# Attention and MoE on one core: the first group's q and k rows, its masks and its weight requests rearranged

## The chip, the cores and the metric

The kernel runs on one core of a Trainium2 chip. The metric is device time in microseconds (us) for one launch, as the median of several runs. Engines are named as the profile names them: PE is TensorE (PEld its weight loads), DVE is VectorE, ACT is ScalarE, POOL is GpSimd, SP is SyncE. POOL and SP, and in the beginning ACT too, also issue transfers (DMAs).

## What is computed

Two steps in a row: attention over 4 batches, 8 heads, 768 tokens and 64 values a head, then a mixture of four experts over the 3072 rows of 512 that come out. Heads 0, 2 and 6 attend to all earlier tokens; heads 1, 3, 4, 5 and 7 attend to the first 4 tokens (sinks) and to a window of 64.

```python
def _attn_ref(q, k, v, is_retrieval, n_sink, window):
    B, H, S, D = q.shape                    # 4, 8, 768, 64
    scores = np.matmul(q, k.transpose(0, 1, 3, 2)) / np.sqrt(D)
    pos = np.arange(S)
    rel = pos[:, None] - pos[None, :]
    causal = rel >= 0
    is_sink = pos[None, :] < int(n_sink)                    # 4
    in_win = (rel >= 0) & (rel < int(window))               # 64
    stream_keep = causal & (is_sink | in_win)
    ...                                     # mask: causal or stream_keep, by head
    a = np.exp(scores - np.max(scores, axis=-1, keepdims=True))
    a = a / (np.sum(a, axis=-1, keepdims=True) + 1e-09)
    return np.matmul(a, v)

def _moe_ref(x, domain_probs, w1, w2):      # x 3072 x 512, w1 4 x 512 x 1024
    p = domain_probs / (domain_probs.sum(-1, keepdims=True) + 1e-09)
    out = np.zeros((N, D))
    for e in range(E):                      # 4 experts
        h = np.maximum(x @ w1[e], 0.0)
        out += p[:, e:e + 1] * (h @ w2[e])
    return out
```

Inputs and output are float32; the kernel computes in fp16 with float32 accumulation.

## The kernel before

Work is cut into eight groups of 384 tokens, half a batch each. For every group the attention runs first and leaves `xT`, the 512 attention values of the group's tokens transposed as four pieces of 128 rows (one for each pair of heads); the MoE of that group reads `xT`. From group 1 on, attention is interleaved with the MoE of earlier groups. Group 0 has nothing to be interleaved with: its attention (`attention(0, 0)`, called "first" in the code) runs alone at the start, and this is the stretch that the change touches. The schedule is manual: each engine executes its instructions in the order in which the source issues them, and Python generators (`yield from`) write that order out. POOL's own order is also the order of the transfers that it requests, as all of them go through one queue.

**Loads of group 0.** The q and k rows of all eight heads come as float32. For each head one DMA of 96 KB brings q and one brings k (L411, L424), in runs of 256 bytes (one row of a head): partition p gets the rows p, 128 + p and 256 + p. SP issues all of k and q of heads 4 to 7; ACT's queue issues q of heads 0 to 3. They land in `hA`, the tile that later holds the hidden layer.

**POOL at the start.** It makes the identity for transposes, requests the values of head 0, and makes the bias masks: `bC` (causal, L457 and L459) and `bS` (window and sinks, three blocks of 160 columns; memset L467, two selects of 2 x 160 columns L468 and L472, small parts L476 to L478, copy of a block L509). Then it requests the values of heads 2, 1, 3, 4, 6, 5 and 7 (`load_v`, L304 for the full heads and L310 for the stream heads), then w1 of expert 0 in two halves of 512 KB (`load_w1`, L335; one half is contraction rows for 64 of the 128 partitions, so every matmul needs both), then w2 of expert 0, and w1 of expert 1. A tiny copy, `landed` (L521), makes POOL wait until a tensor is there; after it come the next q and k rows (L230) and w2 and w1 of the next experts.

**Transposes.** TensorE transposes q and k for each pair of heads `hp` (`transposes(hp)`, heads 2hp and 2hp + 1): three transposes of 128x128 float32 for q, three for k (L576; later groups use pairs of fp16 matmuls with 64 columns, L579). q goes to `qT` by one copy (ACT for the first two pairs, DVE for the others); k goes to `kR` (full heads, L602) or `kS` (stream heads, L618, with the sinks' keys by L626), by DVE. `kS` and `kR` are zeroed first (L379, on DVE).

**Scores and values.** Scores are matmuls (L693), the bias mask is added by a matmul with the identity (L705), ACT takes the exponential into `es` (L711). Values times `es` are matmuls (L756 for full heads, L828 for stream heads), which also give the sums; ACT makes the reciprocal by Ln (L846) and Exp (L856, L861), and DVE multiplies it in (L851), which writes a piece of `xT`. Pairs with a full head go through `x_transposes` (L805, then the copy L809). The order of TensorE in group 0 is

```python
            yield from both(scores(1), values(0))
            yield from transposes(2)
            yield from both(scores(3), values(2))
            x_transposes(0)
            yield from scores(4)
            yield from transposes(3)
            yield from values(1)
            yield from both(scores(5), values(3))
```

after transposes and scores of pairs 0 and 1, and before the scores and values of heads 5, 6 and 7. Matmuls on zeros (`warm_up`, L448) fill some of the waits of TensorE. The first MoE matmuls (L1095, x times w1 of expert 0, pieces of `xT` in the order 0, 2, 1, 3) follow; L1116 is the second layer with w2.

Of the kernel before, what the change touches and what calls it, by code (L numbers as in the profile page):

```python
# [11 lines left out]
FP32 = mybir.dt.float32  # L12
# [7 lines left out]
def kernel(  # L20
# [311 lines left out]
    def load_w1(e, f0, f1):  # L332
        x = moe_w1[e].rearrange("(u c d) f -> u d c f", u=2, c=DMP)
        for u in range(2):
            gp.dma_start(  # L335
                out=w1sb[half(u), e * DMP : (e + 1) * DMP, f0:f1],
                in_=x[u, :, :, f0:f1],
            )
# [42 lines left out]
    def zero(eng, t):  # L381
        fill(eng, t.rearrange("p a b x -> p (a b x)"), 0.0)
# [17 lines left out]
    def rows32(n):  # L400
        x = hA[:, n * 6 * H * D : (n + 1) * 6 * H * D].bitcast(FP32)
        return x.rearrange("p (j h d) -> p j h d", j=3, h=H)
# [3 lines left out]
    for h in range(H):  # L406
        if h == 2:
            nc.sync.dma_start(
                out=v_s32, in_=v[0, :, 0:NS, :].rearrange("h r d -> r h d")
            )  # L410
        nc.sync.dma_start(out=k32[:, :, h, :], in_=rows_of(k, 0, h, 0))  # L411
        if h == HP:

            nc.scalar.add_instruction(
                mybir.InstLoadActFuncSet(
                    name=nc.get_next_instruction_name(),
                    engine=ENG.Activation,
                    act_func_set_id=[x.name for x in SETS].index(
                        "natural_log_exp_and_others"
                    ),  # L420
                )
            )
        eng = nc.scalar if h < HP else nc.sync
        eng.dma_start(out=q32[:, :, h, :], in_=rows_of(q, 0, h, 0))  # L424
# [8 lines left out]
    nc.vector.memset(warm.bitcast(FP32), 0.0)  # L433
    nc.vector.memset(eps, 1e-9)
# [5 lines left out]
    zero(nc.vector, kS[:, 0, :, :, :])  # L440
# [14 lines left out]
    def mask_c(x, keep, drop):  # L455

        gp.memset(x, keep)  # L457
# [7 lines left out]
    def mask_s(x, n, keep, drop):  # L465

        gp.memset(x, keep)  # L467
        gp.affine_select(  # L468
            out=x, in_=x, compare_op=ALU.is_ge, fill=drop,
            base=R0, pattern=[[0, n], [1, TQ]], channel_multiplier=-1,  # L470
        )
        gp.affine_select(  # L472
            out=x, in_=x, compare_op=ALU.is_ge, fill=drop,
            base=NW - 1 - R0, pattern=[[0, n], [-1, TQ]], channel_multiplier=1,
        )
        gp.memset(x[0:R0, :, :], drop)  # L476
        gp.memset(x[0:NS, :, 0:TK], keep)
# [28 lines left out]

    mask_c(bC, 0.0, -60000.0)
    mask_s(bS[:, 0:2, :], 2, 0.0, -60000.0)
    gp.tensor_copy(out=bS[:, 2, :], in_=bS[:, 1, :])  # L509
    load_v(0, 0, [2, 1, 3, 4, 6, 5, 7])  # L510
    load_w1(0, 0, F)
# [46 lines left out]
    def attention(b, c):  # L558
# [8 lines left out]
        def transposed(x, hp):  # L567
# [5 lines left out]
            for j in range(3):  # L573
                o = ps[:, j * P : (j + 1) * P]
                if first:
                    nc.tensor.transpose(o, x[:, j, 2 * hp : 2 * hp + 2, :], ident32)  # L576
                    continue
                for u in range(2):
                    nc.tensor.matmul(  # L579
                        out=o[u * D : (u + 1) * D, :],  # L580
                        lhsT=x[:, 2 * hp + u, j, :],
                        rhs=ident16,
# [5 lines left out]
        def transposes(hp):  # L588
            both_at_once = [] if first else [transposed(x, hp) for x in (qt16, k16)]
            for x, is_k in ((q32 if first else qt16, 0), (k32 if first else k16, 1)):  # L590
                ps = transposed(x, hp) if first else both_at_once[is_k]
# [288 lines left out]
        if first:  # L880
# [8 lines left out]
            sink_row(7)  # L889
            yield from both(scores(1), values(0))  # L890
            yield from transposes(2)
            yield from both(scores(3), values(2))
            x_transposes(0)
            yield from scores(4)
            yield from transposes(3)
            yield from values(1)
            yield from both(scores(5), values(3))
# [770 lines left out]
```

## Time and profile before

| what | value |
|---|---|
| median of 3 runs | 376.53 us (376.28 to 376.87) |
| the profiled execution | 377.82 us, its span 376.1 us |
| granted TensorE clock | 1.00 |
| PE busy | 367.1 us, 98% of the span, 4221 instructions |
| PEld busy | 312.4 us, 83% |
| DVE busy | 281.6 us, 75% |
| ACT busy | 227.3 us, 60% |
| POOL busy | 112.9 us, 30% |
| DMA | 39.25 MB, mean 104 GB/s |

The span is the stretch in which the engines work; the execution's own time lies 1.7 us above it. Times inside a span are counted from its start. "Idle before" in a row is the time that the engine stood still ahead of an instruction, and the arrow names what released it. A row "x3" stands for three neighbours of one line and form. Matmuls are pipelined: one row's time may overlap the next row's start, so the price of a group of matmuls is read from start to start.

### The profile page before, as it was taken

To read this page: it belongs to the slowest core of one execution; us is meant where nothing else is said; L and a number is where in the kernel's file an instruction comes from. 1 tells how busy PE (TensorE), PEld (TensorE's weight loads), DVE (VectorE), ACT (ScalarE), POOL (GpSimd) and SP (SyncE) were. 2 spreads that over 40 slices of the span, in tenths; PEclk is the share of its full clock that TensorE was granted. 3 is DMA by queue.
4 is the path that set the end of the run, shared out by engine and by line. 5 is a ranking of instruction groups with operands and counts; after the bars stand their busy time and mean duration, and the time that the engine had idled before them with its cause. 6 is when DMAs were issued, how large, how long until landed. Compare 5 with 4: busy or idle time off the path is not lost.

```text
span 376.1 us, 10310 instructions
## 1 busy us (share of the span) xinstructions
PE 367.1 (98%) x4221; PEld 312.4 (83%) x4221; DVE 281.6 (75%) x589; ACT 227.3 (60%) x475; POOL 112.9 (30%) x155
## 2 busy tenths in 40 slices
PE   8889999999999999999999999999999999999996
PEld 4755556568998999999989899988899998998996
DVE  7774768697788569868657858957767968989882
ACT  3863478557785785765676955774678362450630
POOL 8923664793058038115601650320000000000000
DMA  8999999999599579988904991971220200300101
GB/s 157 159 208 207 179 186 194 180 201 121 90 104 164 97 83 133 153 111 63 205 12 61 169 156 16 131 129 12 68 72 2 92 24 2 114 2 0 58 3 58
DMA packets 123748, 39.25 MB, mean 104 GB/s; under 512 B 113728, under 2 KB 116356, under 8 KB 123700
## 3 DMA queue, kind: packets, MB, share of 16 engines
q0 software_dynamic: 85824, 19.01, 58.6%
q1 hardware_dynamic: 36276, 19.18, 23.3%
q8 instruction: 33, 0.54, 0.7%
q10 hardware_dynamic: 1600, 0.39, 0.5%
q14 instruction: 15, 0.12, 0.1%
HBM read 44.89 MB, written 6.34 MB: 136 GB/s over the span
## 4 chain that ended last, share of the span: by engine, by line
PE 78%; DMA 12%; DVE 5%; POOL 3%; issue 1%; ACT 0%; DVEq 0%; POOLq 0%
PE pO L1409 29%; PE pA L1229 20%; PE pO L1258 9%; PE pO L1116 5%; DMA q<-in_q_dram 5%; PE pA L693 4%; DMA w2sb<-in_moe_w_dram 4%; PE pA L1095 3%; DMA w1sb<-in_moe_w_dram 2%; PE pV L1258 2%; PE pA L1258 2%; DVE xs L1180 2%; PE pV L828 2%; PE pV L756 2%; DMA xT<-x_pair 1%
## 5 line engine op out<-in xcount | busy, mean ns | idle before, releaser
L1409 PEld LDWEIGHTS <-hA 128*128 128x128 f16 x1104 | 104.9, 98 | 11.9
L1229 PE MATMUL pA<-xs,w1sb 128*128 128x256 f16 x768 | 97.1, 272 | 0.0
L1229 PEld LDWEIGHTS <-w1sb 128*128 128x128 f16 x768 | 71.7, 98 | 7.3
L1409 PE MATMUL pO<-w2sb,hA 128*128 128x256 f16 x640 | 76.8, 272 | 0.0
L711 ACT ACTIVATE es<-pA 128x384 f16<-128x384 f32 (+2 forms) x122 | 59.2, 512 | 26.4 <-PE pA L693 23.2
L1238 ACT ACTIVATE hA<-pA 128x512 f16<-128x512 f32 x96 | 57.2, 597 | 29.6 <-PE pA L1229 27.3
L306 POOL DMA_DIRECT2D vS<-in_v_dram x30 | 29.6, 986 | 113.7 <-PE pV L828 110.5
L1409 PE MATMUL pO<-tsb,hA 128*128 128x256 f16 x464 | 56.8, 272 | 0.0
L1180 DVE TENSOR_TENSOR xs<-xT,pB 128x1024 f16<-128x1024 f16 (+1 forms) x49 | 47.0, 977 | 3.7 <-DMA xT<-x_pair 3.7
L1014 DVE TENSOR_TENSOR hA<-hA 128x1024 f16<-128x1024 f16 x60 | 39.4, 684 | 0.6 <-PE pO L1409 0.3
L1108 ACT ACTIVATE hA<-pA 128x384 f16<-128x384 f32 (+1 forms) x64 | 22.2, 385 | 20.3 <-PE pA L1095 20.2
L1258 PEld LDWEIGHTS <-w1sb 128*128 128x128 f16 x512 | 31.3, 98 | 2.1 <-DVE xs L1014 0.8
L1095 PE MATMUL pA<-xT,w1sb 128*128 128x384 f16 (+1 forms) x256 | 30.4, 272 | 2.0 <-DMA w1sb<-in_moe_w_dram 1.9
L1116 PE MATMUL pO<-w2sb,hA 128*128 128x512 f16 x128 | 30.6, 379 | 0.1
L1095 PEld LDWEIGHTS <-w1sb 128*128 128x128 f16 x256 | 19.5, 98 | 11.0 <-issue 2.6
L1429 ACT COPY s<-pO 128x256 f32<-128x256 f32 x31 | 11.5, 372 | 27.3 <-PE pO L1409 21.8
L851 DVE TENSOR_TENSOR xT<-pV,rc 64x384 f16<-64x384 f32 x37 | 20.5, 554 | 9.3 <-ACT rc L856 6.8
L722 DVE TENSOR_TENSOR es<-es,mS 128x384 f16<-128x384 f16 (+1 forms) x40 | 13.8, 344 | 18.0 <-ACT es L711 17.9
L846 ACT ACTIVATE rc<-pV,eps 64x384 f32<-64x384 f32 x37 | 21.3, 575 | 7.0 <-PE pV L828 6.4
L1275 DVE CUSTOM_DVE_ANT_0 hA<-pO,s 128x512 f16<-128x512 f32 x26 | 17.7, 688 | 9.9 <-PE pO L1258 8.5
L1268 ACT COPY s<-pO 128x512 f32<-128x512 f32 x39 | 22.7, 588 | 3.2 <-PE pO L1258 3.0
L693 PE MATMUL pA<-qT,kR 128*128 128x128 f16 (+2 forms) x141 | 23.1, 261 | 0.4 <-DVE kR L602 0.4
(170 smaller groups left out, 527.6 us busy)
## 6 DMA issues: line engine op xcount, KB each, us to landing
pB<-p_rows SPq DMA_DIRECT2D x10, 512.0 KB
out_dram<-o SPq DMA_DIRECT2D x19, 256.0 KB
w1sb<-in_moe_w_dram POOLq DMA_DIRECT2D x8, 512.0 KB, 9.2
w2sb<-in_moe_w_dram POOLq DMA_DIRECT2D x4, 1024.0 KB, 13.3
vS<-in_v_dram POOLq DMA_DIRECT2D x30, 112.0 KB, 4.8
k_rows<-in_k_dram POOLq DMA_DIRECT2D x18, 128.0 KB, 5.1
q<-in_q_dram POOLq DMA_DIRECT2D x18, 128.0 KB, 6.4
vR<-in_v_dram POOLq DMA_DIRECT2D x24, 48.0 KB, 5.5
```

The lines of the kernel that those rows point to most:

```text
L306: gp.dma_start(out=t[:, :, own_v(h)], in_=windows_of(v, b, h, c))
L693: nc.tensor.matmul(out=ps[:, o : o + nq], lhsT=key_tile(b, c, h, t), rhs=qTs[b, c][:, hp, q0 : q0 + nq], start=(n == 0 or not first), stop ...
L711: nc.scalar.activation(out=es[:, 0:cols], in_=ps[:, 0:cols], func=AF.Exp, scale=SC)
L1014: nc.vector.tensor_tensor(out=out, in0=a, in1=b, op=ALU.subtract)
L1095: nc.tensor.matmul(out=pss[ft][:, 0:cols_n], lhsT=w1_tile(e, ct, ft), rhs=x[:, ct, :], start=(n == 0), stop=(n == DMP - 1),)
L1116: nc.tensor.matmul(out=ps_o, lhsT=hs[:, ft, j * P : (j + 1) * P], rhs=w2sb[:, e * FTP + ft, :], start=(ft == 0), stop=(ft == FTP - 1),)
L1180: nc.vector.tensor_tensor(out=o, in0=xin, in1=pb.to_broadcast([P, DMP, n, P]), op=ALU.mult)
L1229: nc.tensor.matmul(out=ps[:, f * PC : (f + 1) * PC], lhsT=w1_tile(e, ct, f0 + f), rhs=xs[:, ct, :], start=(ct == 0), stop=(ct == DMP - 1),)
L1238: nc.scalar.activation(out=blocks[:, b0 : b0 + 2, k0 : k0 + 2, :].rearrange("p t f x -> p f t x"), in_=ps.rearrange("p (f t x) -> p f t x" ...
L1258: nc.tensor.matmul(out=ps[:, f * P : (f + 1) * P], lhsT=w_tile(e, w[:, ct, :], f), rhs=a[:, ct, :], start=(first and f == 0 and ct == 0), ...
L1268: nc.scalar.copy(out=kept[n], in_=ps)
L1409: nc.tensor.matmul(out=ps, lhsT=a[:, k, :], rhs=b(k), start=(first and k == 0), stop=(k == KT - 1), skip_group_check=not first,)
```

## The change

Four things change, all of them in group 0 or ahead of it.

1. q and k of heads 4 to 7 are loaded two heads at a time (192 KB), so that partition p holds the rows 3p, 3p + 1 and 3p + 2: runs of 768 bytes. SP issues four of these instead of eight loads of 96 KB.
2. Their transposes follow the later groups' form: six matmuls for a tensor, each with one head's 64 columns as weights and the identity as the moving operand, in float32 (plain matmuls, not transposes), the outputs written with a stride of 3. `transposes(hp, 0)` does q alone and `transposes(hp, 1)` k alone, and these halves stand at other places in the order.
3. POOL requests the first half of w1 of expert 0 after the values of heads 2, 1, 3 and 4, then the values of head 6, the second half, and the values of heads 5 and 7.
4. The masks' background is zeroed by one DVE memset (368 float32 columns for `bC` and `bS`), the selects of `bS` work on one block of 160 columns, POOL copies it to the block in front and DVE to the block behind. DVE zeroes `kS` in four pieces.

```diff
--- before.py
+++ after.py
@@ -329,9 +329,9 @@
                 out=vS[0:NS, c, t, :, :], in_=vS[R0 : R0 + NS, 0, 0, :, :]
             )
 
-    def load_w1(e, f0, f1):
+    def load_w1(e, f0, f1, *us):
         x = moe_w1[e].rearrange("(u c d) f -> u d c f", u=2, c=DMP)
-        for u in range(2):
+        for u in us or range(2):
             gp.dma_start(
                 out=w1sb[half(u), e * DMP : (e + 1) * DMP, f0:f1],
                 in_=x[u, :, :, f0:f1],
@@ -399,7 +399,21 @@
 
     def rows32(n):
         x = hA[:, n * 6 * H * D : (n + 1) * 6 * H * D].bitcast(FP32)
-        return x.rearrange("p (j h d) -> p j h d", j=3, h=H)
+        x, y = x[:, 0 : 3 * HP * D], x[:, 3 * HP * D :]
+        x = x.rearrange("p (j h d) -> p j h d", j=3, h=HP)
+        return x, y.rearrange("p (h j d) -> p h j d", j=3, h=HP)
+
+    def load_rows(eng, x, dst, h):
+
+        if h < HP:
+            eng.dma_start(out=dst[0][:, :, h, :], in_=rows_of(x, 0, h, 0))
+            return
+        if h % 2:
+            return
+        eng.dma_start(
+            out=dst[1][:, h - HP : h - HP + 2, :, :].rearrange("p h j d -> p h (j d)"),
+            in_=x[0, h : h + 2, 0:CH, :].rearrange("h (p j) d -> p h (j d)", j=3),
+        )
 
     q32, k32 = rows32(0), rows32(1)
     v_s32 = early[0:NS, 0:1024].bitcast(FP32).rearrange("p (h d) -> p h d", h=H)
@@ -408,7 +422,7 @@
             nc.sync.dma_start(
                 out=v_s32, in_=v[0, :, 0:NS, :].rearrange("h r d -> r h d")
             )
-        nc.sync.dma_start(out=k32[:, :, h, :], in_=rows_of(k, 0, h, 0))
+        load_rows(nc.sync, k, k32, h)
         if h == HP:
 
             nc.scalar.add_instruction(
@@ -421,7 +435,7 @@
                 )
             )
         eng = nc.scalar if h < HP else nc.sync
-        eng.dma_start(out=q32[:, :, h, :], in_=rows_of(q, 0, h, 0))
+        load_rows(eng, q, q32, h)
     nc.sync.dma_start(
         out=probs,
         in_=moe_domain_probs[0 : NPL * P, :].rearrange("(t p) e -> p t e", p=P),
@@ -431,13 +445,15 @@
         in_=moe_domain_probs.rearrange("(t x) e -> t (x e)", x=P),
     )
     nc.vector.memset(warm.bitcast(FP32), 0.0)
+    nc.vector.memset(early[:, 1536:2272].bitcast(FP32), 0.0)
     nc.vector.memset(eps, 1e-9)
     nc.vector.memset(ones, ONES)
     make_identity(nc, ident32)
     one_values(nc.vector, 0)
     load_v(0, 0, [0])
     zero(nc.vector, kR[0][:, 0, :, :, :])
-    zero(nc.vector, kS[:, 0, :, :, :])
+    for t in range(TC):
+        zero(nc.vector, kS[:, 0, t : t + 1, :, :])
     nc.vector.tensor_copy(out=ident16, in_=ident32)
 
 
@@ -452,9 +468,8 @@
 
 
 
-    def mask_c(x, keep, drop):
-
-        gp.memset(x, keep)
+    def mask_c(x, drop):
+
         for i in range(2):
             gp.affine_select(
                 out=x[:, i * P : (i + 1) * P], in_=x[:, i * P : (i + 1) * P],
@@ -462,19 +477,20 @@
                 channel_multiplier=-1,
             )
 
-    def mask_s(x, n, keep, drop):
-
-        gp.memset(x, keep)
+    def mask_s(x, keep, drop):
+
+        y = x[:, 1, :]
         gp.affine_select(
-            out=x, in_=x, compare_op=ALU.is_ge, fill=drop,
-            base=R0, pattern=[[0, n], [1, TQ]], channel_multiplier=-1,
+            out=y, in_=y, compare_op=ALU.is_ge, fill=drop,
+            base=R0, pattern=[[1, TQ]], channel_multiplier=-1,
         )
         gp.affine_select(
-            out=x, in_=x, compare_op=ALU.is_ge, fill=drop,
-            base=NW - 1 - R0, pattern=[[0, n], [-1, TQ]], channel_multiplier=1,
+            out=y, in_=y, compare_op=ALU.is_ge, fill=drop,
+            base=NW - 1 - R0, pattern=[[-1, TQ]], channel_multiplier=1,
         )
-        gp.memset(x[0:R0, :, :], drop)
-        gp.memset(x[0:NS, :, 0:TK], keep)
+        gp.memset(y[0:R0, :], drop)
+        gp.memset(y[0:NS, 0:TK], keep)
+        gp.tensor_copy(out=x[:, 0, :], in_=y)
         gp.affine_select(
             out=x[0:NS, 0, 0:TK], in_=x[0:NS, 0, 0:TK], compare_op=ALU.is_ge,
             fill=drop, base=-NW, pattern=[[1, TK]], channel_multiplier=-1,
@@ -504,11 +520,14 @@
             base=WQ - WF - NW, pattern=[[1, WQ]], channel_multiplier=-1,
         )
 
-    mask_c(bC, 0.0, -60000.0)
-    mask_s(bS[:, 0:2, :], 2, 0.0, -60000.0)
-    gp.tensor_copy(out=bS[:, 2, :], in_=bS[:, 1, :])
-    load_v(0, 0, [2, 1, 3, 4, 6, 5, 7])
-    load_w1(0, 0, F)
+    mask_c(bC, -60000.0)
+    mask_s(bS, 0.0, -60000.0)
+    nc.vector.tensor_copy(out=bS[:, 2, :], in_=bS[:, 1, :])
+    load_v(0, 0, [2, 1, 3, 4])
+    load_w1(0, 0, F, 0)
+    load_v(0, 0, [6])
+    load_w1(0, 0, F, 1)
+    load_v(0, 0, [5, 7])
     load_w2(0)
     zero(gp, kR[0][:, 1, :, :, :])
     zero(gp, kS[:, 1, :, :, :])
@@ -572,22 +591,29 @@
                 ps = pV.tile([P, 512], FP32, name="pV", bufs=2)
             for j in range(3):
                 o = ps[:, j * P : (j + 1) * P]
+                if first and hp < 2:
+                    nc.tensor.transpose(o, x[0][:, j, 2 * hp : 2 * hp + 2, :], ident32)
+                    continue
                 if first:
-                    nc.tensor.transpose(o, x[:, j, 2 * hp : 2 * hp + 2, :], ident32)
-                    continue
+                    o = ps[:, 0:CH].rearrange("r (x j) -> r j x", j=3)[:, j, :]
+                    y = x[1][:, 2 * hp - HP : 2 * hp - HP + 2, :, :]
+                else:
+                    y = x[:, 2 * hp : 2 * hp + 2, :, :]
                 for u in range(2):
                     nc.tensor.matmul(
                         out=o[u * D : (u + 1) * D, :],
-                        lhsT=x[:, 2 * hp + u, j, :],
-                        rhs=ident16,
+                        lhsT=y[:, u, j, :],
+                        rhs=ident32 if first else ident16,
                         start=True,
                         stop=True,
                     )
             return ps
 
-        def transposes(hp):
+        def transposes(hp, *parts):
             both_at_once = [] if first else [transposed(x, hp) for x in (qt16, k16)]
             for x, is_k in ((q32 if first else qt16, 0), (k32 if first else k16, 1)):
+                if parts and is_k not in parts:
+                    continue
                 ps = transposed(x, hp) if first else both_at_once[is_k]
                 if not is_k:
                     op = nc.scalar.copy if first and hp < 2 else nc.vector.tensor_copy
@@ -887,13 +913,15 @@
             sink_row(4)
             sink_row(5)
             sink_row(7)
+            yield from transposes(2, 0)
             yield from both(scores(1), values(0))
-            yield from transposes(2)
+            yield from transposes(2, 1)
             yield from both(scores(3), values(2))
+            yield from transposes(3, 0)
             x_transposes(0)
             yield from scores(4)
-            yield from transposes(3)
             yield from values(1)
+            yield from transposes(3, 1)
             yield from both(scores(5), values(3))
             yield from both(scores(6), values(4))
             yield from both(scores(7), values(6))
```

## The prediction

> **What bounds the kernel now.** The page comes first: TensorE (PE) is busy 98% of 376.1 us at a granted clock of 1.00, so outside group 0 there is little but TensorE work to remove, and the change touches none of that. What it can win are TensorE's waits of the first 55 us. The list of waits of PE in 0:60 (us in total, times, longest):
>
> ```profile
> PE pA L1095 <- DMA w1sb<-in_moe_w_dram: 1.9, 2, 1.1
> PE pV L756 <- ACT es L711: 1.2, 2, 1.0
> PE pA L693 <- DVE kR L602: 0.4, 2, 0.2
> PE pV L579 <- DMA q<-in_q_dram: 0.2, 1, 0.2
> ```
>
> Two waits for w1 make 1.9 us, one for q 0.2. Who made w1 late? The chain of waits over the same stretch (start, length, what), read upwards from the transfer:
>
> ```profile
> 4.25 1.47 POOL early L472
> ...
> 7.03 0.74 POOL vR L304
> 7.76 2.05 POOL vS L310 x3
> 9.81 0.76 POOL vR L304
> 10.57 1.36 POOL vS L310 x2
> 11.93 0.60 POOL w1sb L335
> 12.53 8.84 DMA w1sb<-in_moe_w_dram
> ...
> 22.40 11.30 DMA q<-in_q_dram
> ...
> 41.02 13.57 DMA w2sb<-in_moe_w_dram
> 54.63 1.02 PE pO L1116 x4
> ```
>
> GpSimd (POOL) makes masks, then issues seven value loads, and only then w1. Behind it one stream of transfers (202 to 206 GB/s in the windows between 15 and 40 us) reaches to 54.6 us, where TensorE takes w2 as it lands. Last, TensorE's timeline (start, time, line; in brackets the wait before it):
>
> ```profile
> 9.49 0.30 PE L693 MATMUL pA<-qT,kS 128*128 128x160 f16 x2
> 10.39 0.88 PE L576 MATMUL pA<-early,hA 128*128 128x128 f32 x6
> 12.68 0.82 PE L576 MATMUL pA<-early,hA 128*128 128x128 f32 x6
> 13.33 0.41 PE L828 MATMUL pV<-es,vS 128*128 128x160 f16 x4
> 21.50 5.61 PE L1095 MATMUL pA<-xT,w1sb 128*128 128x384 f16 x32 [1.11 <-DMA w1sb<-in_moe_w_dram]
> 47.85 0.81 PE L1095 MATMUL pA<-xT,w1sb 128*128 128x384 f16 x4 [0.80 <-DMA w1sb<-in_moe_w_dram]
> ```
>
> The attention of group 0 ends near 20.4; the MoE begins at 21.50.
>
> **Earlier weights.** In POOL's timeline the mask work (L457 to L509) lies between 2.40 and 7.03. Removed are two memsets (0.33 and 0.36) and the copy L509 goes to DVE, while a copy of the same 160 columns appears (nothing net). The two selects over 320 columns become 160: rows of one shape read 0.46 and 1.46; halved, they save 0.2 and 0.7, and the narrower fills (0.35 and 0.25) perhaps 0.2. With the gaps between them that is about 2.0 us. Lower bound: L472's 1.46 is a wait behind something else and is paid again, leaving 1.0; upper bound 2.2. One shape at 0.46 and 1.46 needs a cause; DVE's memset of kS (1.12 us from 4.19) ran beside the long one. The Trainium skill ("SBUF — State Buffer", Who interferes with whom) says that VectorE in its two-port modes locks GpSimd out of SBUF; whether this memset is such a mode it does not say. If so, the long select would stay long beside the four pieces of that memset.
>
> With the masks done at 5.0, the value loads of heads 2, 1, 3 and 4 (0.74 and 2.05) end at 7.8; the first half of w1 is requested there (0.6), head 6's values follow (0.76), and the second half goes out from 9.2 to 9.8. Today the halves go out from 11.9 to 13.2. From the second request's start (12.53) to the landing it took 8.84 us; with the same, w1 lands at 9.2 + 8.84 = 18.0, against 21.37. Slowed by the value loads and the rows of q and k still under way, 19.5 is the bad end. Values of heads 5 and 7 now queue behind both halves: needed at 19.09 and 19.66, they land near 19.0, close to the bad side. Everything behind (w2, w1 of expert 1, q and k of the next chunk) comes as much earlier as GpSimd was, about 2 us, bounds 0.5 and 2.5, since the queue is continuous. The waits it removes later: 0.16 at 33.75, 0.80 at 47.85 and about 0.27 at 54.63 (the gap before L1116). Sum 1.2 us, and it takes only 0.8 us of earliness to have it all. The first wait of 1.11 (21.50) goes too, but the three pieces of xT come at 20.99, 21.58 and 22.40 (DVE L809 and L851, behind ACT's L856), so TensorE could start only at about 21.3 without bubbles: 0.2 us. Together 1.4 us faster if group 0 stays as it is.
>
> **Split transposes.** A group of six f32 transposes takes 13.33 − 12.68 = 0.65 us for a q and a k tensor, 0.327 for one: 109 ns each (the first six, at 4.73, took 217 each). After, a tensor of heads 4 to 7 takes six f32 matmuls with 64 weight columns, and no row shows that form. From below: the f16 form of later groups, L579, has six in 0.17 to 0.19 us, two of a pair starting 3 ns apart. From above: six at the 217 ns of the first group, one after the other, 1.30 us. I take 109 ns each without overlap, 0.654, the f32 row being nearest in type; going into and out of the 64-column form cost 0.10 and 0.07 us around L579, so a group costs 0.82 (0.34 to 1.47).
>
> Here the skill speaks against the change. "FP8 and Floating Point Precision", TensorE Precision Notes: true FP32 takes four passes through the array. Four times the f16 pair (4 x 56 ns, three pairs) is 0.67 us, an estimate that agrees with mine if column pairs overlap; if they do not, 1.34 us, and the kernel loses.
>
> Now the walk of TensorE from 9.49, where the order changes: q of heads 4 and 5 (0.82), scores 1 with values 0 (0.67 without its waits), k (0.82), scores 3 with values 2 (0.67), q of heads 6 and 7 (0.75), x_transposes 0.20, scores 4 0.51, values 1 0.25. That is 9.49 + 4.69 = 14.2, against 13.58 today at the same point: 0.6 later, 0.75 with a small slip of DVE. The point matters because ACT's run of Ln and Exp, gapless from 13.78 to 21.81, begins on values 1; whatever delays it delays the xT pieces. The k group of heads 6 and 7 comes after it and is hidden, as TensorE then waits for ACT (1.02 us at 18.36); uncovered it would add 0.82. Loads for these heads: SP issues four of 0.5 us where there were eight (L411 and L424, the last at 8.31); the last leaves near 6.8, so data is early. SP's later issues only move up.
>
> **DVE.** It gets a memset of 368 float columns, 0.37 us by its rows (256 columns 0.27, 384 0.38), the mask copy (0.16), and three more fixed costs of 59 ns for kS in four pieces: about 0.7 us, 0.5 to 0.75. Before L602 at 6.28 it idled 0.77, so this fits at no cost. The copy, however, waits for GpSimd's masks, with the first kR copy queued behind it, and scores 0 behind that; masks end near 5.0, and up to 5.8 it costs nothing, beyond that one for one.
>
> **Sum.** TensorE's MoE begins at 21.3 + 0.65 = 21.95 instead of 21.50: 0.45 lost. The later waits give 1.2. Net 0.8 us. The profiled execution took 377.82 (span 376.1), 1.3 above the median of 376.53; 377.0 there is 375.7 on the scale of the median. With L for how much later values 1 comes, the gain is 1.2 + 0.2 − L, down to L = 1.4, where it is nothing, at a price of about 1.07 us a group.
>
> **Rivals.** A: the forecast, gains of 0.3 to 1.3 us, 375.2 to 376.2, chance 0.40.
>
> B: the split goes like its f16 form (0.34 a group). Against 0.327 today nothing is added, and one group (k of heads 6 and 7) leaves the path: L is about −0.7. Gain 1.4 + 0.7 = 2.1, 374.4. For it, the 3 ns between the two of a pair; against it, an f32 transpose takes 109 ns where an f16 pair takes 56. Chance 0.19.
>
> C, slower: the split f32 matmuls cost 1.30 a group (217 ns each, none overlapping), 1.47 with the switch. Three groups before values 1, 0.65 over the forecast each: L = 0.65 + 1.95 = 2.6, result 1.4 − 2.6 = −1.2, and up to −1.85 if the fourth group finds no cover; I take −1.5, 378.0. It decides from 1.07 a group for no gain and 1.32 for a loss over 0.75. For it: nothing in the trace shows f32 with 64 columns, and the operation is no longer a transpose but a product. Against it: 217 was seen only in the first group, before TensorE had run long. Chance 0.27.
>
> D, nothing to measure: the transfers are no earlier (L472 stays long, w1 slowed by its neighbours), or the values of heads 5 and 7 land at 19.7 and 20.3 behind w1 and stop values 5 and 7 for 0.6; or the copy holds DVE. Gains of 1.4 − 0.65 shrink to 0 to 0.3: 376.4. Chance 0.14.
>
> **Numbers.** About 0.2%, 0.75 us, is what a measurement here can tell from no change. Faster by more: 0.25 of A's 0.40 (its middle is at 0.8), 0.18 of B, 0.02 of D: 0.45. Within: 0.14 of A, 0.01 of B, 0.03 of C, 0.10 of D: 0.28. Slower: 0.01 of A, 0.24 of C, 0.02 of D: 0.27. The range from B's 374.4 to C's 378.0 leaves out half of B and about 0.1 of C, 2 in 10; A's own is 375.2 to 376.2.
>
> **What would show it.** Right: six rows of the split form in 0.6 to 0.9 us; w1 requested by 9.8 and landed by 19.5; no wait for w1 at the first L1095 group nor at 47.85; ACT's Ln of head 1 at 14.3 to 14.6. C shows in rows of over 1 us and the first MoE matmul past 23; B in rows under 0.4; D in waits of L828 for vS or of L602 for POOL. Any wait for the f32 loads at the first split group would prove the walk wrong.

## The result, and the profile after

The changed kernel takes 377.33 us (median of 20 runs, 377.03 to 377.76), the kernel before, run beside it, 376.46 (median of 20, 375.58 to 377.66). The ratio is 1.0018, 95% interval 1.0010 to 1.0026: slower by about 0.7 to 0.9 us, where 0.8 us faster was forecast. The profiled executions say the opposite: the changed kernel's span is 375.3 us (377.03 in all), that of before 376.1 (377.82). Both are correctly read; the contradiction is the subject of what follows. The profiled execution of the kernel after is also the fastest of its 20 runs, that of before slower than all 20 that it is compared with.

TensorE's waits in the first 60 us of the kernel after, to be held against the first fence of the prediction (us in total, times, longest; the row left out is a wait of 1.3 us at the very start, which both kernels have):

```profile
...
PE pV L782 <- ACT es L737: 1.0, 2, 0.8
PE pA L719 <- DVE kR L628: 0.5, 1, 0.5
PE pA L1123 <- DVE xT L835: 0.5, 1, 0.5
PE pA L1123 <- DVE qT L620: 0.3, 1, 0.3
PE pA L1123 <- DVE xT L877: 0.3, 1, 0.3
```

No transfer is in the list any more. The chain of waits no longer runs through GpSimd and the weights, but through TensorE's four split groups (L603; the first and the last are shown) and then ACT and DVE to the last but one piece of `xT` (L877) and the MoE (L1123, which is L1095 of before):

```profile
9.25 0.81 PE pA L603 x12
...
14.25 0.81 PE pA L603 x12
...
21.85 0.57 DVE xT L877
22.46 1.96 PE pA L1123 x11
```

TensorE's timeline has the same (start, time, line, and in brackets the wait ahead):

```profile
9.18 0.88 PE L603 MATMUL pA<-early,hA 128*64 128x128 f32 x12
9.99 0.31 PE L719 MATMUL pA<-qT,kS 128*128 128x160 f16 x2
...
22.46 5.29 PE L1123 MATMUL pA<-xT,w1sb 128*128 128x384 f16 x30 [0.27 <-DVE xT L877]
...
47.29 0.81 PE L1123 MATMUL pA<-xT,w1sb 128*128 128x384 f16 x4
```

Six split matmuls are twelve records, two for each. From the start of a group to the next instruction it is 9.99 − 9.18 = 0.81 us. The first unbroken run of MoE matmuls starts at 22.46, and nothing stands before the row at 47.29, where 0.80 us of waiting stood before. GpSimd's timeline:

```profile
2.92 0.31 POOL L483 TENSOR_SCALAR_AFFINE_SELECT early<-early 128x160 f16<-128x160 f16 x1
3.29 0.32 POOL L487 TENSOR_SCALAR_AFFINE_SELECT early<-early 128x160 f16<-128x160 f16 x1
...
7.60 0.62 POOL L335 DMA_DIRECT2D w1sb<-in_moe_w_dram  x1
...
8.96 0.65 POOL L335 DMA_DIRECT2D w1sb<-in_moe_w_dram  x1
...
18.10 0.18 POOL L540 COPY seen<-w1sb 1x1 f16<-1x1 f16 x1 [1.36 <-DMA w1sb<-in_moe_w_dram]
```

The selects take 0.3 each instead of 0.46 and 1.46, w1 is requested 4.3 and 3.6 us earlier, and it has landed at 18.10 instead of 21.42. The masks, the requests and the landing of w1 came out in the sizes that the prediction worked out.

### The profile page after: what moved, and what is told of

It is laid out like the page before. It is cut to its first block, busy times and chain, and to the rows that moved or that the text cites. A ratio compares the mean times of both kernels' runs of the same rounds, so it can differ in the third digit from the quotient of the medians.

```text
span 375.3 us, 10381 instructions
## 1 busy us (share of the span) xinstructions
PE 367.7 (98%) x4257; PEld 312.9 (83%) x4257; DVE 281.5 (75%) x594; ACT 227.4 (61%) x475; POOL 110.8 (30%) x153
## 4 chain that ended last, share of the span: by engine, by line
PE 92%; DVE 5%; ACT 2%; issue 0%; ACTq 0%
PE pO L1437 31%; PE pA L1257 22%; PE pO L1286 9%; PE pA L1123 7%; PE pO L1144 7%; PE pA L719 5%; PE pV L1286 2%; PE pV L854 2%; PE pV L782 2%; PE pA L1286 2%; ACT es L737 1%; PE pA L603 1%; DVE xs L1208 1%; PE pA L1529 0%; DVE vS L379 0%
## 5 line engine op out<-in xcount | busy, mean ns | idle before, releaser
L1123 PE MATMUL pA<-xT,w1sb 128*128 128x384 f16 (+1 forms) x256 | 30.9, 272 | 1.1 <-DVE xT L835 0.5
L1144 PE MATMUL pO<-w2sb,hA 128*128 128x512 f16 x128 | 30.6, 379 | 0.0
L877 DVE TENSOR_TENSOR xT<-pV,rc 64x384 f16<-64x384 f32 x37 | 20.5, 555 | 10.5 <-ACT rc L882 7.9
L1123 PEld LDWEIGHTS <-w1sb 128*128 128x128 f16 x256 | 19.6, 98 | 10.3 <-issue 2.0
L1457 ACT COPY s<-pO 128x256 f32<-128x256 f32 x31 | 11.5, 372 | 27.3 <-PE pO L1437 21.8
```

The lines of the kernel that those rows point to most:

```text
L1123: nc.tensor.matmul(out=pss[ft][:, 0:cols_n], lhsT=w1_tile(e, ct, ft), rhs=x[:, ct, :], start=(n == 0), stop=(n == DMP - 1),)
L1144: nc.tensor.matmul(out=ps_o, lhsT=hs[:, ft, j * P : (j + 1) * P], rhs=w2sb[:, e * FTP + ft, :], start=(ft == 0), stop=(ft == FTP - 1),)
```

## Is the profile of before the usual case?

Theory 1: the profiled execution of before was an unusual one, with the weights late; most executions have few of the waits that the change removes. Theory 2: the waits are in every execution, and the changed kernel loses its time somewhere that its profile does not show. Two further profiles of the kernel before, unchanged, and an edit that makes its w1 late.

**before_again**, no edit:

> The kernel before, unchanged, for another profile of it. Theory 1 (the profiled execution that the forecast was read from was an unusual one: 377.82 us where the median is 376.46, because the weights came later in it than they mostly do): a span of 374.4 to 375.4, the wait for w1 ahead of the first MoE matmuls under 0.4 us and not 1.11, the wait for w1 near 48 us under 0.4 and not 0.80, all waits for weights and q rows in the first 55 us together 0 to 0.9 us and not 2.1. Theory 2 (those waits are in every execution, and the changed kernel loses its 0.9 us somewhere that its profile does not show): a span near 376 and waits of about 2 us again.

Measured: 376.66 us, ratio 0.9995 (0.9979 to 1.0011), profiled execution 376.34, span 374.6. The shares of its chain by engine, from the page, then its TensorE at the first MoE matmuls and GpSimd's proof that w1 is there:

```profile
PE 87%; DVE 8%; ACT 2%; DMA 1%; issue 1%; DVEq 0%; ACTq 0%
```

```profile
20.88 0.49 PE L1095 MATMUL pA<-xT,w1sb 128*128 128x384 f16 x2 [0.48 <-DMA w1sb<-in_moe_w_dram]
21.64 1.62 PE L1095 MATMUL pA<-xT,w1sb 128*128 128x384 f16 x9 [0.27 <-DVE xT L851]
```

```profile
20.80 0.18 POOL L521 COPY seen<-w1sb 1x1 f16<-1x1 f16 x1 [2.12 <-DMA w1sb<-in_moe_w_dram]
```

In the first profile transfers were 12% of the chain; here they are 1%. w1 has landed 0.6 us earlier, and that is enough: the wait for it (0.48) ends before the pieces of `xT` do, and the unbroken run starts at 21.64 for DVE's piece, not for the weights. The waits at 33.75, 47.85 and 54.63 are not there. Later rows show what that is worth. The group of L1116 that starts at 54.63 in the first profile starts here, and then in the kernel after (as L1144), at

```profile
53.42 1.02 PE L1116 MATMUL pO<-w2sb,hA 128*128 128x512 f16 x4
```

```profile
54.22 1.02 PE L1144 MATMUL pO<-w2sb,hA 128*128 128x512 f16 x4
```

So the kernel after is 0.41 us ahead of the first profile of before and 0.80 us behind before_again: the sign of the change depends on which profile of before is taken.

**before_third**, no edit, one run:

> The kernel before once more, for a third profile. Theory 1: w1 landed between 20.3 and 21.0, waits for weights under 0.5 us in the first 55 us, span 374.2 to 375.2. If the first profile was the usual case: w1 at 21.4, waits of 2 us, span 376.

Measured: 376.46 us, span 374.8, w1 landed at 20.84, no wait for a weight in the first 55 us, though one of 0.34 us for a row of q at 5.20; the same group of L1116 starts at 53.93. Two profiles of three lie near the median of 376.46 and have none of the three later waits; the one that the prediction read is above all 20 of the timed runs of its comparison. Such executions are rare but not unique: of all 122 timed runs of the kernel before, four took 377.82 us or more.

**w1_late**, GpSimd's zeroing of 1.2 us put ahead of the request of w1:

```diff
+    zero(gp, kS[:, 1, :, :, :])
     load_w1(0, 0, F)
     load_w2(0)
     zero(gp, kR[0][:, 1, :, :, :])
-    zero(gp, kS[:, 1, :, :, :])
```

> The kernel before with GpSimd's zeroing of kS (1.2 us) moved ahead of the request of w1. Theory 1: in most executions of the kernel before, w1 comes 0.2 to 0.8 us before it would stop TensorE (landed at 20.8 where the first whole group can start at 21.6), so 1.2 us of lateness cost 0.5 to 1.3 us: 376.8 to 377.6, and its profile shows the waits of the first profile again (0.5 to 1.5 us at the first MoE matmuls). Theory 2 (the waits are always there): the full 1.2 us and more, 377.5 to 378.5.

Measured: 377.2 us, ratio 1.0025 (1.0015 to 1.0034), within the first range, but not by the waits expected. In the profile w1 was requested 1.1 us later (13.01) and landed at 21.05, inside the 20.80 to 21.42 of the three profiles of before. TensorE waited for no weight; the MoE came late (22.24) because DVE stood still in three small casts (1.86 us, L318), of which more below. So it does not weigh the waits.

## What the parts of the change do

**split_only**, the 768-byte rows, split matmuls and the new order; masks and requests as before (the diff is against the kernel after):

```diff
-    mask_c(bC, -60000.0)
-    mask_s(bS, 0.0, -60000.0)
-    load_v(0, 0, [2, 1, 3, 4])
-    load_w1(0, 0, F, 0)
...
+    mask_c(bC, 0.0, -60000.0)
+    mask_s(bS[:, 0:2, :], 2, 0.0, -60000.0)
+    load_v(0, 0, [2, 1, 3, 4, 6, 5, 7])
+    load_w1(0, 0, F)
```

> Of the change only the 768-byte rows, their split f32 transposes and the order on TensorE; masks and requests stay as in the kernel before. Theory 1: 0.5 us more for each of three groups that stand before the values of head 1, less the fourth that is taken from there, 0.7 to 0.9 us later at the first MoE matmuls: 377.1 to 377.5, with a spread of single runs as in the kernel before. Theory 2: the same 0.9 us plus what the profile does not show, 378.0 or more.

Measured: 377.39 us, 1.0021 (1.0003 to 1.0038). That is inside the range of theory 1. All of the loss is in this part; the earlier weights and masks do nothing to the median on top of it (377.33), although w1 still stops TensorE once in this profile, for 0.31 us at 48.16. What they would be worth without the loss is not measured by itself: with 256-byte rows they bring a loss of their own (below).

**after_values_first**, the kernel after with all value loads ahead of w1:

```diff
-    load_v(0, 0, [2, 1, 3, 4])
-    load_w1(0, 0, F, 0)
-    load_v(0, 0, [6])
-    load_w1(0, 0, F, 1)
-    load_v(0, 0, [5, 7])
+    load_v(0, 0, [2, 1, 3, 4, 6, 5, 7])
+    load_w1(0, 0, F)
```

> The changed kernel with all value loads ahead of w1, as in the kernel before (w1 requested from about 9.7 and not from 7.6). Theory 1: w1 still lands before 20.5 where the first whole MoE group starts at 22.5, so its place buys nothing: 377.1 to 377.5, the changed kernel's time. Theory 2 (the early request is worth about a microsecond): 378 or more.

Measured: 377.06 us, 1.0020 (1.0004 to 1.0035). w1 landed at 18.81 instead of 18.10, and the unbroken MoE run started at 22.46 as before. Where w1 stands among the value loads buys nothing, as theory 1 has it.

**double_q2**, one group of the kernel after done twice:

```diff
                 ps = transposed(x, hp) if first else both_at_once[is_k]
+                if parts == (0,) and hp == 2:
+                    ps = transposed(x, hp)
```

> The changed kernel with the six split matmuls of q of heads 4 and 5 done twice. Theory 1: 0.8 us more on TensorE ahead of the values of head 1, which nothing hides: MoE 0.7 to 0.8 later, 378.0 to 378.2. Theory 2: the group is not on the path, under 0.3 us more: 377.3 to 377.6.

Measured: 377.87 us, 1.0041 (1.0028 to 1.0055), about 0.5 more than the kernel after in the medians, 0.7 in the spans of the profiles (376.0 against 375.3); ACT's first Ln came at 15.26 instead of 14.61 and the MoE run at 23.12 instead of 22.46. Doing the group twice adds 0.65 us on TensorE (24 records from 9.18, the next instruction at 10.64 instead of 9.99), so in these two profiles all that was added lies on the path; the other 0.16 of the 0.81 us is paid once, for six matmuls as for twelve. By its median the run lies between the two theories, nearer to the first.

**f16_triples**, the price of the split form taken down: q and k of heads 4 to 7 cast to fp16 by GpSimd's transfer.

```diff
+    for x, y in ((q, q32[1]), (k, k32[1])):
+        gp.dma_start(out=y.rearrange("p h j d -> p h (j d)"),
+            in_=x[0, HP:H, 0:CH, :].rearrange("h (p j) d -> p h (j d)", j=3))
     load_v(0, 0, [2, 1, 3, 4])
...
-                        rhs=ident32 if first else ident16,
+                        rhs=ident16,
```

> The changed kernel with q and k of heads 4 to 7 cast to fp16 by the transfer (two requests of GpSimd, 0.75 us each, ahead of the values of head 2), so that the split groups use fp16 matmuls with the same 64 columns. Everything else stays. Theory 1 (the 0.8 us that values of head 1 come later are the price of the split float32 form, 0.81 us a group): a group costs 0.17 to 0.36, values 1 and the MoE come 1.3 to 1.5 us earlier than in the changed kernel, w1 (requested 1.5 us later) lands near 19.5 and holds nothing: 375.7 to 376.1. Theory 2 (what makes the changed kernel late is not the split form but the new places in the order and the traffic of the early weights): 377.0 to 377.6, about the changed kernel's time.

Measured: 376.24 us, 0.9998 of before (0.9987 to 1.0008), 1.1 us under the kernel after. TensorE's rows:

```profile
9.18 0.52 PE L602 MATMUL pA<-ident,hA 128*64 128x128 f16 x6
9.63 0.31 PE L718 MATMUL pA<-qT,kS 128*128 128x160 f16 x2
...
20.32 0.42 PE L853 MATMUL pO<-es,vS 128*128 128x160 f16 x4 [1.32 <-DMA vS<-in_v_dram]
```

A group costs 0.45 from start to start and not 0.81 (0.17 to 0.36 was expected), and ACT's Ln starts at 13.54 and not at 14.61: 1.07 us earlier, where three groups of 0.36 us less make 1.08. The order is that of the kernel after, so theory 2 is out. The gain is partly lost again: values of head 5, requested behind both halves of w1, stop TensorE for 1.32 us, and the time is 0.14 above the range of theory 1.

**f16_values_first** (the first part of the diff), and **f16_x_late** (both parts):

```diff
-    load_v(0, 0, [6])
+    load_v(0, 0, [6, 5, 7])
     load_w1(0, 0, F, 1)
-    load_v(0, 0, [5, 7])
...
-            x_transposes(0)
             yield from scores(4)
             yield from values(1)
+            x_transposes(0)
```

> The fp16 triples with the values of heads 5 and 7 requested ahead of the second half of w1. Theory 1: the wait of 1.3 us for vS at values 5 goes; ACT's run starts at 13.5 as in the fp16 triples, 0.25 before that of the kernel before, w1 (second half from 11.8) lands by 20.8, and the first whole group of MoE matmuls starts near 21.4: 375.9 to 376.2, with profiled spans of 374.2 to 374.5. Its rival: the second half of w1 is now the last to come and takes back what the values gave, 376.2 to 376.6.

> As the run before, and x_transposes of head 0 moved behind scores 4 and values 1. If TensorE's order ahead of values 1 is what starts ACT's run, it starts 0.2 to 0.3 us earlier, 375.6 to 375.9, as far as w1 is there; if w1 ends last, no change against the run before.

Measured: 376.03 us, 0.9997 (0.9984 to 1.0010), and 375.92 us, 0.9993 (0.9984 to 1.0001). Both beat the kernel after by 1.3 to 1.4 us in the medians; against the kernel before even the second is not separated from no change. ACT's first Ln comes at 13.38 in it, 0.16 earlier than in f16_triples, where 0.2 to 0.3 was expected. Its MoE run starts at 21.25, 0.39 before that of before_again. The profile of f16_values_first happened to be one of its two late runs in twelve (378.03, where ten lie between 375.7 and 376.34):

```profile
PE pA L1121 <- DMA w1sb<-in_moe_w_dram: 1.3, 2, 1.1
...
PE pO L1142 <- DMA w2sb<-in_moe_w_dram: 0.7, 1, 0.7
```

They stand at 20.39, 47.50 and 54.89, near the places of the waits of the first profile of before, and here too in a run 2 us above its own median.

## Early weights beside 256-byte rows

**weights_only**, masks and early w1 of the change with the rows, transposes and order of before:

```diff
-    load_v(0, 0, [2, 1, 3, 4, 6, 5, 7])
-    load_w1(0, 0, F)
+    load_v(0, 0, [2, 1, 3, 4])
+    load_w1(0, 0, F, 0)
+    load_v(0, 0, [6])
+    load_w1(0, 0, F, 1)
+    load_v(0, 0, [5, 7])
```

> Of the change only the masks and the earlier request of w1 (and the zeroing that belongs to them); rows of q and k, their transposes and the order on TensorE stay as in the kernel before. Theory 1: most executions of the kernel before have few of the waits that this removes, so the gain over its median is 0 to 0.5 us (376.0 to 376.4), and the times of single runs spread less. Theory 2: the 1.4 us of waits go in every run: 375.0 to 375.2.

**weights_order**, the same with the new places of the half groups, unsplit:

```diff
+            yield from transposes(2, 0)
             yield from both(scores(1), values(0))
-            yield from transposes(2)
+            yield from transposes(2, 1)
             yield from both(scores(3), values(2))
+            yield from transposes(3, 0)
             x_transposes(0)
             yield from scores(4)
-            yield from transposes(3)
             yield from values(1)
+            yield from transposes(3, 1)
```

> The change without its 768-byte rows: masks, requests and the new places of the four half groups of transposes, but these as three 128-column f32 transposes from 256-byte rows, 0.33 us a half group. Theory 1: values of head 1 come 0.3 us earlier than in the kernel before and ACT's run with them, so 0.3 to 0.6 us faster than weights alone: 375.5 to 376.0. Theory 2: 374.7 to 374.9. Either way faster than both kernels, if the rows of heads 4 and 5 are there at 9.2 us; if they are not, a wait for hA shows at that group and the gain shrinks by it.

Measured: 381.22 us, 1.0112 (1.0082 to 1.0143), and 382.23, 1.0135 (1.0093 to 1.0178). Neither theory foresaw it. DVE's timeline of weights_only shows one thing, its transfers between 12 and 16 us (queue: packets, MB, share) another:

```profile
9.21 3.25 DVE L318 CAST vS<-early 4x256 f16<-4x256 f32 x3
```

```profile
...
q1 hardware_dynamic: 734, 0.08, 28.4%
```

The three casts of sinks take 3.25 us and not 0.8. And q1, SP's queue, still carries rows of q and k after 12 us: the last of them landed at 15.29, against 10.64 to 11.47 in the three profiles of before and 10.17 in the kernel after, which has longer runs and half as many loads for heads 4 to 7.

**masks_only** (masks new, all value loads ahead of w1), **masks_sinks** (its three casts moved behind `x_transposes(0)`) and **masks_act** (the casts on ACT, in the diff) ask for the casts:

```diff
-            sink_row(4)
-            sink_row(5)
-            sink_row(7)
             yield from both(scores(1), values(0))
+            sink_row(4, nc.scalar.copy)
             yield from transposes(2)
             yield from both(scores(3), values(2))
+            sink_row(5, nc.scalar.copy)
             x_transposes(0)
             yield from scores(4)
+            sink_row(7, nc.scalar.copy)
```

> The kernel before with the new masks alone: GpSimd is free 2.2 us earlier, but all seven value loads still go ahead of w1, which is requested at about 9.7 and not at 7.6. Theory 1 of the 256-byte rows (w1 beside rows that are still under way stops them: with w1 from 7.6 the last rows of q and k come near 16): here w1 starts when most rows have landed, so the last group of float32 transposes waits at most 0.5 us; 376.2 to 376.6, single runs within 1 us of one another. Its rival (any earlier transfers of GpSimd stop the rows): 378 or more.

> Masks alone, with the three small DVE casts of the sinks of heads 4, 5 and 7 (one took 2.5 us there instead of 0.27, beside GpSimd's requests) moved behind the copy of x_transposes of head 0. If DVE stood still because these casts meet GpSimd's requests, the stall shrinks or goes: 376.0 to 376.8, no single run over 378. If DVE is held by the 256-byte rows that are landing at the same time, whatever it executes, the stall shows at another instruction and the time stays at 378 or more.

> Masks alone, with the sink casts of heads 4, 5 and 7 on ACT instead of DVE (0.3 to 0.4 us each, at places where ACT waits for scores). If it is these casts on DVE that stand still beside GpSimd's requests, nothing on DVE takes over 0.6 us between 9 and 15 us any more, and the time falls from 378.4 to 376.2 to 376.8. If the 256-byte rows or the requests hold up whatever DVE executes, another instruction takes 1 to 2.5 us and the time stays over 377.5.

Measured: 378.39 us (1.0061, 1.0034 to 1.0088), 377.15 (1.0034, 1.0022 to 1.0046), 376.55 (0.9998, 0.9980 to 1.0016). DVE's row in masks_only:

```profile
9.09 3.38 DVE L318 CAST vS<-early 4x256 f16<-4x256 f32 x3
```

The second of its three took 2.51 us. The time is that of the rival (378 or more), but not for its reason: the rows landed at 11.67 in masks_only and at 12.00 in masks_act, which loses nothing. Moved, the three casts still took 2.04 us, from 13.54, after the last row (11.11) and beside GpSimd's memsets; the time came between the two forecasts. On ACT the stall is gone from DVE and the 1.8 us of loss with it, as forecast. So it is these casts on DVE. Masks_only also has rows that land 3.6 us earlier than in weights_only, and the two differ only in where w1 stands among the requests (9.71 or 7.60): the early w1 is what holds the rows up.

**weights_act**, weights_only with the casts on ACT:

> Masks and early weights without the 768-byte rows, and the same three casts on ACT. The stall of the casts goes (2 us of the 4.8 that this variant lost); the rows of heads 6 and 7, which landed at 15.3 beside w1 instead of 10.6 to 11.4, still stop the last group of transposes: 378.5 to 380. If the stall was all, 376.2 to 376.8; if the rows were all, 381 as before.

Measured: 381.22 us (1.0113, 1.0076 to 1.0150), as weights_only and as forecast for the case that the rows were all: the casts were late in the shadow of the rows.

```profile
16.91 1.51 PE L581 MATMUL pA<-early,hA 128*128 128x128 f32 x6 [4.49 <-issue]
```

TensorE stands for 4.49 us ahead of the last group of transposes, whose rows landed at 15.6. The label names no releaser; that the rows ended the wait is read from when they landed. A second thing adds to the loss. The page of this run gives the granted clock of TensorE, in tenths, over 40 slices of the span:

```profile
PEclk9789999999999999999999999999999999999999
```

It was 0.81 from 12 to 16 us, 0.50 from 16 to 20 and 0.83 from 20 to 24, where before_again has 1.00 throughout, and the six transposes took 1.51 us where they take 0.82 in before_again. ACT's first Ln comes at 18.94, 5.16 after that of before, 0.92 more than the transposes' own delay of 4.24 against before_again. The profiles of weights_only, weights_order and masks_only show such a stretch as well, and the four timed runs of the three variants with early weights whose mean clock was 0.999 or 1.000 took 378.48 to 380.25. So the 4.8 us are the wait for the rows and a slower clock that begins within it; how much is which in the median is not separated, nor is it tested whether the wait brings the slower clock.

**k3_late**, masks_only with the k half of the last group later:

```diff
+            yield from transposes(3, 0)
             yield from scores(4)
-            yield from transposes(3)
             yield from values(1)
+            yield from transposes(3, 1)
```

> Masks alone as in the run before, and the k half of the last group of transposes moved behind the values of head 1 (three 128-column transposes, 0.33 us). ACT's run of Ln and Exp is what the first MoE matmuls wait for, so they come 0.3 us earlier: 375.9 to 376.2 where masks alone give 376.2 to 376.6. If w1 or DVE ends last there instead, no gain.

Measured: 377.01 us, 1.0019 (1.0004 to 1.0035). That is above both its ranges. The casts stood still in it too (0.81 and 1.32 us), so it puts no price on the order, though it beats masks_only by 1.4.

## Why the prediction was wrong

**The step that failed** is "Earlier weights", where 1.11 + 0.16 + 0.80 + 0.27 us of waits were taken as the kernel's own, and its consequence in the sum, "the later waits give 1.2" and "377.0 there is 375.7 on the scale of the median". The profiled execution lay 1.3 us above the median. The prediction saw that, and carried the 1.3 through as a constant. But those 1.3 us were the waits (their worth was put at 1.4): in an execution at the median they are not there (before_again and before_third), so nothing can be won from them. What is left of its sum is the loss alone, slower instead of faster: with its own L of 0.65 the sum gives 376.46 + 0.65 = 377.1, with the 0.83 of the two profiles 377.3; measured 377.33. That the second fits to a tenth is partly luck, because L was larger still (below).

**The split groups were right.** 0.82 us forecast, 0.81 measured; double_q2 (dearer) and f16_triples (cheaper) show from both sides that their price is on the path. The Trainium skill ("FP8 and Floating Point Precision", TensorE Precision Notes) speaks of four passes for true FP32; the estimate of 0.67 us from it, plus the switch of 0.17, is 0.84 if the pairs overlap, and the measured 0.81 agrees with that and not with its other case of 1.34. The prediction's own reading, six matmuls of 109 ns without overlap, gives the same sum; the row of twelve records does not tell the two apart. Neither rival B (0.34 a group) nor C (1.47) came.

**L was 0.83, not 0.65, and 1.2 where like is compared with like.** ACT's first Ln stands at 14.61 against 13.78 (first before, then after):

```profile
13.78 0.58 ACT L846 ACTIVATE rc<-pV,eps 64x384 f32<-64x384 f32 x1 [0.35 <-PE pV L828]
```

```profile
13.87 0.71 ACT L737 ACTIVATE es<-pA 128x320 f16<-128x320 f32 x2 [1.02 <-PE pA L731]
14.61 0.58 ACT L872 ACTIVATE rc<-pV,eps 64x384 f32<-64x384 f32 x1
```

The prediction let it wait for values 1, which came at 13.83, earlier than its 13.9. But with the k group moved away, scores 4 and values 1 are neighbours, and ACT first has the exponentials of scores 4 to do (13.87 to 14.58). What starts ACT's run is now scores 4, at 13.33 where it was at 12.17; the k group never stood ahead of that, and the q group of heads 6 and 7 was moved there. The fourth group was hidden, as forecast. ACT's run is not quite gapless, as the prediction calls it: it waits 0.22 us at 18.85 and 0.30 at 19.54 for TensorE, and the same in the kernel after, so that the delay goes through undiminished.

The walk of TensorE was also longer than its sum, 5.00 us (9.18 to 14.18) and not 4.69; it reached the forecast 14.2 by luck, as it began 0.31 earlier than 9.49. That start is not the change's. It goes back to the first six transposes, which differ between executions: 1.51 us in the first profile of before, 0.84 in w1_late, whose code is the same up to there. The profile of the kernel after has the short form, that of split_only the long one, like before:

```profile
4.83 0.84 PE L595 MATMUL pA<-early,hA 128*128 128x128 f32 x6
```

```profile
4.72 1.52 PE L590 MATMUL pA<-early,hA 128*128 128x128 f32 x6
...
15.01 0.58 ACT L867 ACTIVATE rc<-pV,eps 64x384 f32<-64x384 f32 x1
```

In split_only Ln comes 1.23 after that of before, and the unbroken MoE run at 22.86, 1.22 after that of before_again. So L was put at about half its size. The medians lose less, 0.87 (kernel after) and 0.98 (split_only, against the 376.41 beside it); why is not shown.

**Right as well:** masks 2.2 us shorter (2.0 forecast), w1 landed at 18.1 (18.0), no wait for the values of heads 5 and 7, none for the f32 rows. Why L472 took 1.46 us stays open: in the kernel after the selects are over (3.61) before DVE zeroes `kS` (from 4.38). Rival D has the right shape (no gain from the weights, 0.65 lost), but as a mishap of transfers, and it adds up to 376.4; by the number alone 377.33 is nearer to C's 378.0, whose cause did not come.

**That DVE's new work "fits at no cost"** holds only beside long first transposes. In the profile of the kernel after TensorE waits 0.53 us for DVE's first copy (`kR`, L628). In w1_late, with the short transposes and the DVE work of before, that copy starts at 5.55 and the first scores at 6.16; in the kernel after they start at 5.94 and 6.48, 0.32 us later (6.48 again in double_q2, whose first transposes start at 4.62, against 4.67 in w1_late).

**What the prediction did not see at all** is why the parts belong together: the 768-byte rows gain nothing themselves, but without them the early weights cost 4.8 us, of which a part is a slower TensorE clock.

## What to carry to other kernels

When the profiled execution lies above the median by about as much as the waits that a change is to remove, the waits may be what sets that execution apart: look for a second profile, or count only what is sure to be in the median. A transfer that lands within about a microsecond of its use can be a wait in one execution and none in another (one of the three profiles of before). Here, making it earlier went with a narrower spread of the times (0.7 us over 20 runs of the kernel after, 1.35 over 12 of split_only) and left their middle where it was (377.33 and 377.39). The kernel before spread over 2.1 us in 20 runs, but over 1.0 in the 12 of before_again, so the spread is the weaker finding. And where an order is changed, ask anew which instruction starts the engine that sets the end: it was the values before and the scores after.

## What the runs showed of the hardware

- A group of six float32 matmuls with 64 weight columns costs 0.81 us, six fp16 ones in the same place 0.45, three 128-column f32 transposes 0.33. Six more directly behind add 0.65 (double_q2). Each f32 matmul of this form leaves two records.
- The first six f32 transposes of the kernel took 1.51 us in one execution and 0.84 in another, with the same code up to there (before and w1_late).
- Rows of 256 bytes on SP's queue that are under way when 1 MB of weights is requested on GpSimd's wait for it: the last landed at 15.3 to 15.6 (weights_only, weights_order, weights_act), instead of 10.6 to 11.5 in before and 11.7 where w1 came 2.1 us later (masks_only). With 768-byte runs in half as many loads it was 10.2, with the same early weights; the length of the runs and the number of loads were not separated.
- The granted clock of TensorE fell within a wait of 4.49 us and was 0.50 from 16 to 20 us (weights_act); with a wait of 2.15 us it stayed at 1.00 (masks_sinks).
- A DVE cast of 4x256 from float32 to fp16, both in SBUF, took 0.27 to 2.5 us beside GpSimd's requests, and 1.14 beside its memsets (the first of the three in masks_sinks). The Trainium skill ("SBUF — State Buffer", Who interferes with whom) counts casts among what can contend with GpSimd, the second to come standing until the first is done; that the loss went when ACT did the casts agrees with it. But 2.5 us is longer than any request under way there (0.62 to 0.79), and the same casts passed in 0.27 to 0.6 beside the same requests in the kernels before and after. Nor is it the instructions ahead of them: in w1_late the three took 1.86 us, and there all that is issued ahead of them is as in before. What decides between the two was not found.
